# Bigbird attention and a top-2 mixture of experts in one kernel: zero fills moved to the middle batches, listed v rows by byte offset, keys issued ahead of values

## The chip, the cores and the metric

The kernel runs on one core of a Trainium2 chip. The metric is device time in microseconds (us) of one execution. Three timed runs of the kernel before stand beside one profiled execution; the profile's clock of TensorE is the granted one, as a share of full speed (2.4 GHz; the lower level is 1.2 GHz, 0.50).

## The reference

```python
def _attn_ref(q, k, v, sampled_blocks):            # B, H, S, D = 4, 8, 768, 64; 24 blocks of 32
    scores = scale * np.matmul(q, k.transpose(0, 1, 3, 2))
    mask = np.abs(blk_i - blk_j) <= window             # window = 1 block
    mask = mask | (blk_i == 0) | (blk_j == 0) | (blk_i == n_blocks - 1) | (blk_j == n_blocks - 1)
    for qb in range(n_blocks):
        for kb in sampled_blocks[qb]:                  # 3 listed blocks for each query block
            mask[qb * block:(qb + 1) * block, kb * block:(kb + 1) * block] = True
    ...                                                # masked softmax, then attn @ v

def _moe_ref(x, w_gate, w_noise, noise, w1, w2):       # N, D, E, F = 3072, 512, 8, 1024
    noisy_logits = x @ w_gate + np.log1p(np.exp(x @ w_noise)) * noise
    ...                                                # top 2 of 8 experts, softmax of the two
    h = np.maximum(x[mask] @ w1[e], 0.0)
    out[mask] += top2_w[mask, k, None] * (h @ w2[e])
```

The attention's output, 4 batches x 768 rows of 512 numbers, is the input x of the experts.

## The kernel before, in words

**Attention.** A batch b has 6 tiles t of 128 query rows, and each tile has two items f (four heads each); four more items "g" of a batch serve the first and the last block, which see everything. `steps()` walks 64 items in a software pipeline: in one step it scores the item two ahead (PE L238, then max and exp on DVE and ACT), turns the present one (PE transposes, L304), multiplies the one before with v (`av`, PE L326), and makes the output rows of the one before that (`high` on ACT L383, `low` on POOL L390). Two steps later `turn_x` transposes these rows on PE (L397). Rows of the first and last tile of a batch (x tile `xe`) also need the "g" result: POOL makes its low half (`xg`, L371), DVE copies it into `xe` (L376), and PE turns `xe`.

Every engine executes its instructions in the order in which the program writes them; nothing reorders them later. What sets the order is the code of `steps()`, and a table `plan` by step number, in which the last batch's extra work and the experts' first loads are put.

**Queues.** SP issues all plain DMAs, in program order. The DMAs use eight completion semaphores in turn (DMAHW0 to DMAHW7), and each waits for the one eight issues before it, which had the same semaphore. For each tile (b, t) SP issues: the query tile q (256 KB), a store of finished x rows (256 KB, L589, it waits for POOL's `low`), a TENSOR_LOAD of the listed block numbers into registers (L155), and in two halves the tile's v: one DMA of window rows per half (`vw`, up to 384 KB, L212) and the listed rows, 64 KB each (L216; 12 to a tile, 9 for t = 0 and 5). Half 1 of a tile is written one step behind half 0. v lies in three buffers (`va`, `vb`), two in the last batch; a tile's DMAs wait until PE's `av` of the buffer's last user is done. Ahead of every listed DMA stands register arithmetic (the "ISA" rows below, FUSED_REGOPS in the trace) that makes an address of a block number.

POOL does, in one stream: `weigh` (L224: two small copies of `known` into the columns of va and vb behind the 512 v columns), `prefetch_k` (kc copies L196 and L197: listed and neighbouring key blocks of a tile, which `scores` reads), `scale_k` (L176, each sixth of the next batch's keys kk), `low`, and all indirect DMAs. `load_k` (SP L164) brings the next batch's keys in six pieces.

**Zero fill.** The output is built by scattered additions, so 8 DMAs of 768 KB (L1284) fill it with zeros. They are in the plan at steps 49 to 57, in the last batch; their source is x tile 2, which POOL clears for it, and then a piece of `xg` of the experts.

**Experts.** Behind the attention come units of up to 816 token rows (expert products L1006, L1045, L1092, L1101). Rows are gathered by POOL (L948), transposed by SP's DMA (`xpose`, L958), and the running output is gathered too (`gather_prev`, POOL L966). Unit 0's gathers and transposes begin inside the last batch's steps.

Of the kernel before, what the change touches and what calls it, by code (L numbers as in the profile page):

```python
# [9 lines left out]
F32 = mybir.dt.float32  # L10
# [3 lines left out]
U32 = mybir.dt.uint32  # L14
U16 = mybir.dt.uint16
AF = mybir.ActivationFunctionType
ALU = mybir.AluOpType
AX = mybir.AxisListType
PSUM = bass.MemoryType.PSUM
P = 128  # L20
# [7 lines left out]
C = 816  # L28
# [5 lines left out]
OVC = OVT * P  # L34
NSLOT = NV * OVC
BIGIDX = 1 << 20
EW = 8
NC = E * EW
SW = 16384.0
FAST = 5  # L40
# [6 lines left out]
class Attention:  # L47
# [3 lines left out]
    def __init__(self, tc, qt, qg, kt, vx, vw, vg, sampled, H, D):  # L51
        self.tc, self.nc = tc, tc.nc
        self.qt, self.qg, self.kt, self.vx, self.vw, self.vg, self.sampled = qt, qg, kt, vx, vw, vg, sampled
        self.B, self.T = qt.shape[:2]
        self.H, self.D = H, D
        self.NP = H // 2
        self.S = self.T * P
        self.NB = self.S // 32
        self.W = D + 4
        self.HD = H * D  # L60
        self.HW = H * self.W
        self.late_ = (self.B - 1) * self.T
        self.items = []
        for b in range(self.B):
            q = [("q", b, t, f) for t in range(self.T) for f in range(2)]
            g = [("g", b, i, par) for i in range(2) for par in range(2)]
            self.items += g[0:2] + q[0:1] + g[2:3] + q[1:2] + g[3:] + q[2:] if b == 0 else q[0:1] + g[0:3] + q[1:2] + g[3:] + q[2:]
        self.st = {}

    def open(self, ctx, early, ident):  # L70
        tc, nc = self.tc, self.nc
# [12 lines left out]
        J = self.NJ  # L84
# [12 lines left out]
        nc.vector.tensor_copy(self.ident16, self.ident)  # L97
        nc.vector.memset(self.known, 1.0 / XS)

    def open_x(self, ctx):  # L100
# [9 lines left out]
    def blocks(self, mi):  # L110
        nc, NB = self.nc, self.NB
# [4 lines left out]
        t = lambda name, dt=F32, n=3: mi.tile([1, NB, n], dt, name=name)  # L116
        r = t("rf")
# [7 lines left out]
        bi = mi.tile([1, NB], F32, name="bi")  # L125
        nc.gpsimd.iota(bi, pattern=[[1, NB]], base=0, channel_multiplier=0, allow_small_or_imprecise_dtypes=True)
        u, w = t("du"), t("dw")
        nc.vector.tensor_tensor(u, r, bi[:, :, None].to_broadcast([1, NB, 3]), op=ALU.subtract)
# [9 lines left out]
        self.mi = self.const.tile([1, NB * 3], I32, name="mr")  # L138
        nc.vector.tensor_tensor(self.mi.rearrange("p (b k) -> p b k", k=3), r, w, op=ALU.subtract)
        ones = mi.tile([1, P], F32, name="on")  # L140
# [60 lines left out]
    def prefetch_v(self, b, t, half):  # L201
        nc, HD, J = self.nc, self.HD, self.NJ
        i = self.which(b, t)
        va, vb = self.va[i], self.vb[i]
        self.st["v", b, t] = va, vb
        js = self.real(t)
        first = t * J + js[0]
        if half == 0:
            self.unlisted = self.numbers(self.mi[0:1, 3 * first:3 * (first + len(js))], mybir.EngineType.SP, self.NB)
        js = [j for j in js if j // 2 == half]  # L210
        part = lambda x: x.rearrange("p (j c) -> p j c", j=J)[:, js[0]:js[-1] + 1]
        nc.sync.dma_start(va[0:96, js[0]:js[-1] + 1, 0:HD], part(self.vw[b, t]))  # L212
        vv = self.vx[b].rearrange("(n p) c -> n p c", p=32)
        for j in js:
            for n, d in enumerate((va[96:128, j], vb[0:32, j], vb[32:64, j])):
                nc.sync.dma_start(d[:, 0:HD], vv[bass.ds(self.unlisted[3 * (t * J + j - first) + n], 1)].rearrange("o p c -> (o p) c"))  # L216

# [213 lines left out]
    def steps(self, router, done, background):  # L431
# [7 lines left out]
        for k in range(-2, n + 7):  # L439
# [37 lines left out]
            if new[0] == "q" and new[1] + 1 < B:  # L477
                i = 2 * new[2] + new[3] - 1
                if i == 2:
                    self.load_g(new[1] + 1)  # L480
                    self.load_ends(new[1] + 1)
                if 2 <= i <= 7:
                    self.scale_k(new[1] + 1, i - 2, 6, nc.gpsimd)
            if new[0] == "q" and new[3] == 1 and nk < len(tg):
# [13 lines left out]
            while nv < len(tg) and (self.after(nv) < 0 and k > 0 or old[0] == "q" and old[3] == 1 and  # L498
# [5 lines left out]
                nv += 1  # L504
            if new[0] == "q" and new[1] + 1 < B and 0 < 2 * new[2] + new[3] <= 6:
                self.load_k(new[1] + 1, 2 * new[2] + new[3] - 1, 6)
            background(k, 3)
# [284 lines left out]
class Experts:  # L792
# [167 lines left out]

    def gather_prev(self, u):
        nc = self.nc
        r = self.st["u", u]
        for c in () if self.plain(u) else self.chunks(u):
            m = self.rows_of(u, c)
            nc.gpsimd.indirect_dma_start(  # L966
                out=self.pv[0:m, c, :], out_offset=None, in_=self.out,
                in_offset=bass.IndirectOffsetOnAxis(ap=r["gi"][0:m, c:c + 1], axis=0),
                bounds_check=self.N - 1, oob_is_err=False)
# [275 lines left out]
@with_exitstack  # L1245
def kernel(ctx, tc, qt, qg, kt, vx, vw, vg, sampled_blocks, gates, noise, w1, w2, out):
    nc = tc.nc
# [9 lines left out]
    ex = Experts(tc, router, w1, w2, out, x_dram)  # L1257
    att = Attention(tc, qt, qg, kt, vx, vw, vg, sampled_blocks, H, DM // H)
    late, early, left, right, first = (ExitStack() for _ in range(5))
# [18 lines left out]

    def spare():
        return att.xs[2].rearrange("p n a c -> p (n a c)")[:, 0:512].bitcast(F32)  # L1280

    def fill_out(i):
        z = spare() if i < 4 else ex.xg[:, C // P, 0:512].bitcast(F32)
        nc.sync.dma_start(out[i * 384:(i + 1) * 384].rearrange("(p n) (h d) -> p (n h) d", p=P, d=256),  # L1284
                          z[:, None, :].to_broadcast([P, 3 * DM // 256, 256]))

# [5 lines left out]

    at(PER * 3 + 1, lambda: nc.gpsimd.memset(spare(), 0.0))
    for i in range(8):
        at(PER * 3 + 1 + i + i // 4, fill_out, i)
    for i in range(3):
# [65 lines left out]
    def front(u, f):  # L1362
# [29 lines left out]
        if u >= FAST - 1:  # L1392
            e = ex.units[u][1]
            if u == FAST - 1:
                for c in ((0, 1), (2, 3), (4, 5), (6,))[f] if f < 4 else ():
                    ex.xpose(u + 1, c)
            do(u, FRONT[f])
            if nn:
                do(u, FRONT_ROWS[f])
# [47 lines left out]
    for u in range(nu):  # L1447
        left_ = ex.rows(u)[1]
        n = ex.count(u)
        ex.layer1(u, lambda f: front(u, f))  # L1450
        for k, c in enumerate(ex.chunks(u)):
            ex.mm2(u, c)
            if left_ and k == min(2, n - 1):
                ex.turn(u, n - 1)
            back(u, k, n)
        if u + 1 < nu:
            ex.gather_prev(u + 1)
        if u == 2:
            second.close()
            ex.open_sums(right)  # L1460
# [4 lines left out]

_INS = ['qt', 'qg', 'kt', 'vx', 'vw', 'vg', 'sampled_blocks', 'gates', 'noise', 'moe_w1', 'moe_w2']
_OUTS = [((3072, 512), 'float32')]
# [46 lines left out]
```

## Time and profile before

| | us |
|---|---|
| three runs | 861.11, 861.96, 867.26 (median 861.96) |
| the profiled execution | 867.49 |
| its span | 865.6 |
| PE busy in the span | 795.9 (92%) |
| DVE, ACT, POOL busy | 567.7, 388.4, 375.2 |
| mean granted clock | 0.959 |

Read it as two programs one behind the other: the attention with the router up to 318.68 us of the span, where the chain of work shows the first expert product (L1006), and then the experts, in which PE hardly stops. The change touches DMAs and small instructions of the first part. There PE's gaps, what ended each of them, and the time at which SP and POOL come to the work that PE waits for are what is to be read.

### The profile page before, as it was taken

How to read it: one execution, taken by the hardware profiler on the slowest of the kernel's cores; microseconds unless marked ns; L12 is line 12 of the kernel's file. 1: busy time of each engine (PE TensorE's matmuls, PEld its weight loads, DVE VectorE, ACT ScalarE, POOL GpSimd, SP SyncE). 2: the span in 40 equal slices, each digit the busy share in tenths (PEclk: the TensorE clock that was granted, in tenths of full speed). 3: DMA queues.
4: the chain of work that ended last, by engine and by line, in shares of the span. 5: the costliest groups of instructions: out<-in, count | busy, mean ns of one | idle time of the engine just before them, and what ended most of it. 6: DMA issues, size and time to landing. Idle time of an engine off the chain costs nothing.

```text
span 865.6 us, 25234 instructions
## 1 busy us (share of the span) xinstructions
PE 795.9 (92%) x9823; PEld 488.4 (56%) x9823; DVE 567.7 (66%) x1197; ACT 388.4 (45%) x722; POOL 375.2 (43%) x656
## 2 busy tenths in 40 slices
PE   8999789988967759999999879999999999999996
PEld 4566557666646547466586444554554554554552
DVE  7767767798797418752133268688698697796631
ACT  5869738858744325321023222552552542633510
POOL 5584379388554230141235316516426336322311
PEclk8999989999988769999999979999999999999999
DMA  7776676786688876764179939639639539523301
GB/s 226 205 209 179 200 202 186 201 233 192 213 246 271 208 173 171 195 185 96 52 174 208 188 102 235 203 97 228 190 105 237 185 100 242 164 79 117 102 28 52
DMA packets 119844, 148.88 MB, mean 172 GB/s; under 512 B 69516, under 2 KB 76301, under 8 KB 119715
## 3 DMA queue, kind: packets, MB, share of 16 engines
q1 hardware_dynamic: 107490, 109.22, 47.8%
q0 software_dynamic: 12224, 37.96, 13.9%
q8 instruction: 79, 1.29, 0.7%
q14 instruction: 51, 0.41, 0.2%
HBM read 107.28 MB, written 26.15 MB: 154 GB/s over the span
## 4 chain that ended last, share of the span: by engine, by line
PE 75%; DVE 9%; issue 6%; SPq 2%; DMA 2%; POOL 2%; ACT 2%; POOLq 1%; DVEq 0%; ACTq 0%
PE pc L1092 29%; PE pa L1045 10%; PE ps L238 6%; PE pa L1006 6%; PE pd L1045 5%; PE po L326 4%; PE pd L1006 3%; PE ps L304 3%; PE pc L1101 3%; PE pc L1045 2%; DVE m L277 2%; SPq L958 1%; PE po L349 1%; PE ps L292 1%; PE po L397 1%
## 5 line engine op out<-in xcount | busy, mean ns | idle before, releaser
L1092 PE MATMUL pc<-w,hh 128*128 128x512 f16 x768 | 228.4, 379 | 0.0
L1125 POOL DMA_INDIRECT out_dram<-y,r_xT x46 | 66.4, 1444 | 216.0 <-DVE y L1124 182.6
L1092 PE MATMUL pc<-w,hl 128*128 128x512 f16 x384 | 145.5, 379 | 0.0
L1092 PEld LDWEIGHTS <-hh 128*128 128x128 f16 x768 | 74.5, 98 | 86.4
L1045 PEld LDWEIGHTS <-w 128*128 128x128 f16 x840 | 82.2, 98 | 63.1
L280 ACT ACTIVATE p<-ps,m 128x256 f32<-128x256 f32 x192 | 75.2, 477 | 55.6 <-DVE m L277 54.9
L277 DVE TENSOR_REDUCE m<-ps 128x2 f32<-128x512 f32 x96 | 61.7, 684 | 32.3 <-PE ps L238 32.3
L1014 ACT ACTIVATE hh<-pa 128x408 f16<-128x408 f32 (+2 forms) x60 | 26.3, 447 | 123.2 <-PE pa L1006 111.9
L196 POOL COPY kc<-kk 128x128 f32 x264 | 68.1, 295 | 15.0 <-PE ps L238 7.7
L238 PE MATMUL ps<-kc,q 64*32 64x256 f32 x1536 | 64.3, 404 | 10.0 <-POOL kc L197 8.2
L896 DVE SCALAR_TENSOR_TENSOR w<-wraw,w 128x1024 f16<-128x1024 f32 (+1 forms) x58 | 65.3, 1128 | 10.5 <-ACT w L892 10.5
L326 PE MATMUL po<-va,ptr 128*32 128x68 f32 x1536 | 56.9, 233 | 13.2 <-DMA va<-in_vx_dram 9.6
L1017 DVE SCALAR_TENSOR_TENSOR hl<-pa,hh 128x408 f16<-128x408 f32 (+2 forms) x60 | 30.2, 504 | 54.1 <-ACT hh L1014 54.1
L948 POOL DMA_INDIRECT xg<-x_rows,r_xT x46 | 57.6, 1253 | 14.7 <-issue 14.4
L1092 PEld LDWEIGHTS <-hl 128*128 128x128 f16 x384 | 37.5, 98 | 45.3
L966 POOL DMA_INDIRECT pv<-out_dram,r_xT x44 | 48.0, 1090 | 32.9 <-issue 26.3
L326 PE MATMUL po<-vb,ptr 128*32 128x68 f32 x1536 | 55.0, 230 | 6.4 <-issue 5.4
L892 ACT ACTIVATE w<-wraw 128x1024 f16<-128x1024 f32 (+1 forms) x58 | 56.4, 975 | 6.7 <-DMA wraw<-in_moe_w_dram 6.7
L1124 DVE SCALAR_TENSOR_TENSOR y<-pc,r_xT,pv 128x512 f32<-128x512 f32 x37 | 27.8, 750 | 47.3 <-PE pc L1092 47.3
L326 PEld LDWEIGHTS po<-va,ptr 128*32 128x32 f32 x1536 | 39.2, 114 | 27.7 <-DMA va<-in_vw_dram 10.1
L304 PE MATMUL ps<-r_ident,p 128*128 128x128 f32 x384 | 54.6, 287 | 0.0
L1006 PE MATMUL pd<-xta,w 128*128 128x408 f16 (+1 forms) x144 | 46.8, 333 | 8.3 <-DVE hl L1017 8.2
(230 smaller groups left out, 1593.1 us busy)
## 6 DMA issues: line engine op xcount, KB each, us to landing
wraw<-in_moe_w_dram SPq DMA_DIRECT2D x64, 512.0 KB, 3.8
va<-in_vw_dram SPq DMA_DIRECT2D x40, 384.0 KB, 4.5
vb<-in_vx_dram SPq DMA_DIRECT2D x176, 64.0 KB, 3.1
q<-in_qt_dram SPq DMA_DIRECT2D x24, 256.0 KB, 3.5
va<-in_vx_dram SPq DMA_DIRECT2D x88, 64.0 KB, 3.5
kk<-in_kt_dram SPq DMA_DIRECT2D x18, 256.0 KB, 3.2
x_rows<-x SPq DMA_DIRECT2D x16, 256.0 KB, 4.2
out_dram<-x SPq DMA_DIRECT2D x4, 768.0 KB, 7.6
```

The costliest lines, as they stand in the source:

```text
L196: nc.gpsimd.tensor_copy(kc[:, j, :, 3 + n], flat[:, bass.ds(self.listed(blk, n), P)].rearrange("p (n c) -> p n c", c=32))
L238: mm = lambda o, l, r: nc.tensor.matmul(o, l, r, start=True, stop=True, skip_group_check=True)
L277: nc.vector.tensor_reduce(m[:, par], s[par].rearrange("p (e c) -> p e c", e=2), axis=AX.X, op=ALU.max, negate=True)
L280: nc.scalar.activation(p[:, 2 * e + par], s[par][:, 256 * e:256 * e + 256], AF.Exp, bias=m[:, par, e:e + 1])
L304: nc.tensor.transpose(t[:, e, c], p[:, 2 * e + par, P * c:P * c + P], self.ident)
L326: nc.tensor.matmul(o[32 * j:32 * j + 32, h], d[:, h % 2, h // 2, x, 32 * j:32 * j + 32], self.values(v[:, self.slot(t, j)], 4 * f + h), st ...
L896: self.nc.vector.scalar_tensor_tensor(lo, t, WS, hi, op0=ALU.mult, op1=ALU.subtract)
L948: nc.gpsimd.indirect_dma_start(out=self.xg[0:m, c + self.place(u)], out_offset=None, in_=self.x_dram[0:nr], in_offset=bass.IndirectOffsetO ...
L1006: nc.tensor.matmul(ph[:, 0:m], w[:, wt, slot, kb % 2 * P:kb % 2 * P + P], r["xt"][:, kb, a, o:o + m], start=i == 0, stop=i == last)
L1045: nc.tensor.matmul(o, w[:, wt, slot, s * P:s * P + P], mv(s, a), start=i == 0 and p in tail, stop=i == 5, skip_group_check=True)
L1092: nc.tensor.matmul(py, h[:, f, o], w(f)[:, x], start=i == 0, stop=i == last)
L1125: d = nc.gpsimd.indirect_dma_start(out=self.out, out_offset=bass.IndirectOffsetOnAxis(ap=r["ix"][0:m, c:c + 1], axis=0), in_=y[0:m], in_of ...
```

## The change

- The 8 zero fills go from steps 49 to 57 to steps 19, 22, ..., 40 (batches 1 and 2), one every third step. Their source is a new tile `zero` that DVE clears once at the start.
- Listed v rows are addressed by byte offsets. The numbers that SP loads are already block x 65,536; v comes as one tensor per batch (vx0 to vx3), and source and target of the DMA are seen as bytes (`bitcast(U8)`).
- The numbers that SP loads for tiles t = 3, 4 and 5 stay in registers over the batches (KEEP), so 9 of 24 TENSOR_LOADs go.
- `load_k` is written ahead of the step's v instead of behind it, and `scale_k` one step later (i - 3 in place of i - 2).
- Unit 4's `gather_prev` is written inside the loop of unit 4's front work rather than behind the previous unit.

```diff
+        self.RB = 32 * self.HD * 4
+        self.held_v = {}
...
+        self.zero = self.const.tile([P, 256], F32, name="zero")
+        nc.vector.memset(self.zero, 0.0)
...
-        nc.vector.tensor_tensor(self.mi.rearrange("p (b k) -> p b k", k=3), r, w, op=ALU.subtract)
+        nc.vector.scalar_tensor_tensor(self.mi.rearrange("p (b k) -> p b k", k=3), w, -float(self.RB), rb, op0=ALU.mult,
+                                       op1=ALU.add)
...
         if half == 0:
-            self.unlisted = self.numbers(self.mi[0:1, 3 * first:3 * (first + len(js))], mybir.EngineType.SP, self.NB)
+            self.unlisted = self.held_v.get(t)
+            if self.unlisted is None:
+                self.unlisted = self.numbers(self.mi[0:1, 3 * first:3 * (first + len(js))], mybir.EngineType.SP,
+                                             self.NB * self.RB)
+                if t in KEEP:
+                    self.held_v[t] = self.unlisted
...
-        vv = self.vx[b].rearrange("(n p) c -> n p c", p=32)
+        rows = self.vx[b].rearrange("s c -> (s c)").bitcast(U8)
         for j in js:
             for n, d in enumerate((va[96:128, j], vb[0:32, j], vb[32:64, j])):
-                nc.sync.dma_start(d[:, 0:HD], vv[bass.ds(self.unlisted[3 * (t * J + j - first) + n], 1)].rearrange("o p c -> (o p) c"))
+                at = self.unlisted[3 * (t * J + j - first) + n]
+                nc.sync.dma_start(d[:, 0:HD].bitcast(U8), rows[bass.ds(at, self.RB)].rearrange("(p c) -> p c", p=32))
...
                 i = 2 * new[2] + new[3] - 1
+                if 0 <= i < 6:
+                    self.load_k(new[1] + 1, i, 6)
...
-                if 2 <= i <= 7:
-                    self.scale_k(new[1] + 1, i - 2, 6, nc.gpsimd)
+                if 3 <= i <= 8:
+                    self.scale_k(new[1] + 1, i - 3, 6, nc.gpsimd)
...
-            if new[0] == "q" and new[1] + 1 < B and 0 < 2 * new[2] + new[3] <= 6:
-                self.load_k(new[1] + 1, 2 * new[2] + new[3] - 1, 6)
...
     def fill_out(i):
-        z = spare() if i < 4 else ex.xg[:, C // P, 0:512].bitcast(F32)
...
-                          z[:, None, :].to_broadcast([P, 3 * DM // 256, 256]))
+                          att.zero[:, None, :].to_broadcast([P, 3 * DM // 256, 256]))
...
-    at(PER * 3 + 1, lambda: nc.gpsimd.memset(spare(), 0.0))
     for i in range(8):
-        at(PER * 3 + 1 + i + i // 4, fill_out, i)
+        at(PER + 3 + 3 * i, fill_out, i)
...
+                if f > 3:
+                    ex.gather_prev(u, ex.chunks(u)[2 * f - 8:2 * f - 6])
...
-        if u + 1 < nu:
+        if u + 1 < nu and u + 1 != FAST - 1:
             ex.gather_prev(u + 1)
```

Two places show how instructions stand. The first is POOL at the turn from batch 0 to batch 1: `weigh` (L224, COPY va and vb) for tiles (1, 0), (1, 1) and (1, 2), between them `low` of the last rows of batch 0 (L390) and `xg` (L371), with the semaphores that each waits for. Before:

```order
L224 COPY va_96<-known 128x3x32
L224 COPY vb_99<-known 128x3x32
L390 TENSOR_TENSOR x_978<-xr,x_978 128x2x128 [waits Activation_49] x2
L224 COPY va_97<-known 128x4x32 [waits PE_49]
L224 COPY vb_100<-known 128x4x32 [waits PE_49]
L390 TENSOR_TENSOR xe<-xr,xe 128x2x128 [waits Activation_49] x2
L371 TENSOR_TENSOR xg<-xr,xg 128x2x128 [waits DVE_49,Activation_49]
L224 COPY va_98<-known 128x4x32 [waits PE_49,Pool_49]
L224 COPY vb_101<-known 128x4x32 [waits PE_49,Pool_49]
```

The same place in the changed kernel (weigh is L239 there, low L405, xg L386):

```order
L239 COPY va_96<-known 128x3x32 [waits DMAHW7_49,DMAHW4_49]
L239 COPY vb_99<-known 128x3x32 [waits DMAHW5_49,DMAHW6_49,DMAHW1_49,DMAHW0_49]
L405 TENSOR_TENSOR x_981<-xr,x_981 128x2x128 [waits Activation_49] x2
L239 COPY va_97<-known 128x4x32 [waits DMAHW4_49,DMAHW7_49,DMAHW0_49,PE_49]
L239 COPY vb_100<-known 128x4x32 [waits DMAHW2_49,DMAHW5_49,DMAHW1_49,DMAHW6_49,DMAHW0_49,PE_49]
L405 TENSOR_TENSOR xe<-xr,xe 128x2x128 [waits Activation_49] x2
L386 TENSOR_TENSOR xg<-xr,xg 128x2x128 [waits DVE_49,Activation_49]
L239 COPY va_98<-known 128x4x32 [waits DMAHW6_49,DMAHW3_49,DMAHW7_49,PE_49,Pool_49]
L239 COPY vb_101<-known 128x4x32 [waits DMAHW4_49,DMAHW1_49,DMAHW5_49,DMAHW0_49,DMAHW7_49,PE_49,Pool_49]
```

The order is unchanged; what is new is that both copies of each `weigh` wait for DMAs of SP: seen as bytes, the listed rows' target counts as touching the columns that `weigh` writes, so it waits for the listed rows of both halves of its own tile. The same holds for every tile of every batch.

The second place is SP between the last listed row of tile (1, 2) and the first of (1, 3), around the keys (kk) of batch 2. Before:

```order
L216 ISA
L216 DMA vb_101<-in_vx_dram 32x512 [waits DMAHW0_49]
L164 DMA kk_102<-in_kt_dram 128x512 [waits DMAHW1_49]
L589 DMA x_rows<-xe 128x1024 [waits DMAHW2_49,DVE_49]
L589 DMA x_rows<-xe 128x1024 [waits DMAHW3_49,DVE_49,Pool_49]
L187 DMA q<-in_qt_dram 128x512 [waits DMAHW4_49,PE_49]
L164 DMA kk_102<-in_kt_dram 128x512 [waits DMAHW5_49]
L169 DMA qg_106<-in_qg_dram 128x256 [waits DMAHW6_49]
L172 DMA ends_108<-in_vg_dram 64x512 [waits DMAHW7_49]
L155 TENSOR_LOAD mr
L212 DMA va_96<-in_vw_dram 96x2x512 [waits DMAHW0_49,PE_49]
```

And in the changed kernel:

```order
L231 DMA vb_101<-in_vx_dram 32x2048 [waits DMAHW0_49]
L173 DMA kk_102<-in_kt_dram 128x512 [waits DMAHW1_49]
L604 DMA x_rows<-xe 128x1024 [waits DMAHW2_49,DVE_49]
L604 DMA x_rows<-xe 128x1024 [waits DMAHW3_49,DVE_49,Pool_49]
L1295 DMA out_dram<-zero 768x1x256 [waits DMAHW4_49]
L173 DMA kk_102<-in_kt_dram 128x512 [waits DMAHW5_49]
L196 DMA q<-in_qt_dram 128x512 [waits DMAHW6_49,PE_49]
L173 DMA kk_102<-in_kt_dram 128x512 [waits DMAHW7_49]
L178 DMA qg_106<-in_qg_dram 128x256 [waits DMAHW0_49]
L181 DMA ends_108<-in_vg_dram 64x512 [waits DMAHW1_49]
L226 DMA va_96<-in_vw_dram 96x2x512 [waits DMAHW2_49,PE_49]
```

The arithmetic row ahead of each listed DMA and this tile's TENSOR_LOAD are gone, the first zero fill has come in, and a third piece of kk stands ahead of the v of (1, 3). On POOL the first `scale_k` of batch 2's keys now stands behind the kc copies of tile (1, 3), where it stood ahead of them. POOL's rows from the last batch's steps on are in the same order in both kernels, the `gather_prev` of unit 4 included; so are all of PE's and ACT's, while DVE has two instructions more.

## Rows read from the trace of the kernel before

**Rows 1.** Chain of waits, 290 to 325 us (start, length, what)

```profile
296.31 2.04 SPq L958
...
298.45 1.27 SPq L958
...
301.63 3.13 DMA vb<-in_vx_dram
...
318.68 0.42 PE pa L1006
```

**Rows 2.** Timeline of PE, attention (start, us, engine, line, operation [idle before <-releaser])

```profile
86.14 0.28 PE L397 MATMUL po<-a_ident,xe 128*128 128x128 f16 x2 [0.67 <-DVE xe L376]
...
109.40 3.07 PE L238 MATMUL ps<-kc,q 64*32 64x256 f32 x32 [6.90 <-POOL kc L197]
...
163.05 0.82 PE L397 MATMUL po<-a_ident,xe 128*128 128x128 f16 x8 [0.67 <-DVE xe L376]
...
231.91 0.28 PE L397 MATMUL po<-a_ident,xe 128*128 128x128 f16 x2 [0.67 <-DVE xe L376]
...
292.96 0.40 PE L326 MATMUL po<-va,ptr 128*32 128x68 f32 x2 [5.68 <-DMA va<-in_vx_dram]
293.64 0.32 PE L326 MATMUL po<-va,ptr 128*32 128x68 f32 x1 [0.28 <-DMA va<-in_vx_dram]
...
304.89 0.26 PE L326 MATMUL po<-vb,ptr 128*32 128x68 f32 x2 [0.88 <-DMA vb<-in_vx_dram]
```

**Rows 3.** Waits, 0 to 330 us (us in total, times, longest)

```profile
POOL kk L176 <- DMA kk<-in_kt_dram: 35.7, 9, 13.8
...
PE po L326 <- DMA va<-in_vx_dram: 9.6, 4, 5.7
```

**Rows 4.** Busy time, granted clock and DMA share by stretch

```profile
100.00:110.00 10.00, 3.10 (x100) 2.08 (x84) 6.05 (x36) 3.69 (x9) 4.76 (x17) 0.75 0.78 222
```

**Rows 5.** Line L216, whole run (xcount: duration ns min/median/max, first and last start)

```profile
L216 SPq DMA_DIRECT2D vb<-in_vx_dram x176: 315/316/1822, 8.5 to 301.6; - x176
```

**Rows 6.** Timeline of SP, around tiles (3, 1) and (3, 4)

```profile
227.40 0.83 SPq L216 DMA_DIRECT2D vb<-in_vx_dram  x2
...
277.04 0.36 SPq L589 DMA_DIRECT2D x_rows<-x  x1
280.62 0.34 SPq L212 DMA_DIRECT2D va<-in_vw_dram  x1
```

**Rows 7.** Line L155, whole run

```profile
L155 SPq TENSOR_LOAD <-mr x24: 745/1023/3427, 5.2 to 290.3; - x24
```

**Rows 8.** Line L1284, the zero fills, whole run

```profile
L1284 SPq DMA_DIRECT2D out_dram<-xg x4: 552/576/1126, 252.8 to 275.8; - x4
...
DMA to landing us min/median/max: 5.2/6.4/7.6
```

**Rows 9.** Line L216, end of tile (1, 1)

```profile
L216 SPq DMA_DIRECT2D vb<-in_vx_dram x6: 315/320/1122, 85.5 to 91.0; - x6
...
DMA to landing us min/median/max: 1.8/1.9/1.9
```

**Rows 10.** Timeline of POOL, turn to batch 1 and last batch

```profile
74.31 0.29 POOL L224 COPY va<-known 128x128 f32<-128x128 f32 x1
...
83.67 0.67 POOL L371 TENSOR_TENSOR xg<-xr,xg 128x256 f16<-128x256 f32 x1 [1.71 <-ACT xg L370]
...
275.34 1.26 POOL L948 DMA_INDIRECT xg<-x_rows,r_gi  x1 [0.18 <-issue]
```

**Rows 11.** Line L216, end of tile (2, 1)

```profile
L216 SPq DMA_DIRECT2D vb<-in_vx_dram x6: 315/316/1047, 155.9 to 160.8; - x6
...
DMA to landing us min/median/max: 2.4/2.7/3.2
```

**Rows 12.** DMA issues, 262 to 306 us (KB each, median us to landing)

```profile
vb<-in_vx_dram SPq DMA_DIRECT2D x22, 64.0 KB, 4.7
...
xg<-x_rows,r_gi POOLq DMA_INDIRECT x5, 6.1
```

More of the change, by code (lines that the diff above doesn't have):

```diff
@@ L15 @@
 U16 = mybir.dt.uint16
+U8 = mybir.dt.uint8
 AF = mybir.ActivationFunctionType
@@ L35 @@
 NSLOT = NV * OVC
+KEEP = (3, 4, 5)
 BIGIDX = 1 << 20
@@ L126, in blocks @@
         nc.gpsimd.iota(bi, pattern=[[1, NB]], base=0, channel_multiplier=0, allow_small_or_imprecise_dtypes=True)
+        rb = t("rb")
+        nc.vector.tensor_scalar(rb, r, float(self.RB), None, op0=ALU.mult)
         u, w = t("du"), t("dw")
@@ L959, in xpose, with gather_prev @@
                                          in_=self.xg[:, c + self.place(u)])
-    def gather_prev(self, u):
+    def gather_prev(self, u, some=None):
         nc = self.nc
         r = self.st["u", u]
-        for c in () if self.plain(u) else self.chunks(u):
+        for c in () if self.plain(u) else (some or self.chunks(u)):
             m = self.rows_of(u, c)
@@ L1245, with kernel @@
 @with_exitstack
-def kernel(ctx, tc, qt, qg, kt, vx, vw, vg, sampled_blocks, gates, noise, w1, w2, out):
+def kernel(ctx, tc, qt, qg, kt, vx0, vx1, vx2, vx3, vw, vg, sampled_blocks, gates, noise, w1, w2, out):
     nc = tc.nc
@@ L1257 @@
     ex = Experts(tc, router, w1, w2, out, x_dram)
-    att = Attention(tc, qt, qg, kt, vx, vw, vg, sampled_blocks, H, DM // H)
+    att = Attention(tc, qt, qg, kt, (vx0, vx1, vx2, vx3), vw, vg, sampled_blocks, H, DM // H)
     late, early, left, right, first = (ExitStack() for _ in range(5))
@@ L1277 @@
     UB = 9
-    def spare():
-        return att.xs[2].rearrange("p n a c -> p (n a c)")[:, 0:512].bitcast(F32)
     def fill_out(i):
-        z = spare() if i < 4 else ex.xg[:, C // P, 0:512].bitcast(F32)
         nc.sync.dma_start(out[i * 384:(i + 1) * 384].rearrange("(p n) (h d) -> p (n h) d", p=P, d=256),
-                          z[:, None, :].to_broadcast([P, 3 * DM // 256, 256]))
+                          att.zero[:, None, :].to_broadcast([P, 3 * DM // 256, 256]))
     plan = {}
@@ L1463 @@
     overflow(tc, router, w1, w2, out, x_dram, table)
-_INS = ['qt', 'qg', 'kt', 'vx', 'vw', 'vg', 'sampled_blocks', 'gates', 'noise', 'moe_w1', 'moe_w2']
+_INS = ['qt', 'qg', 'kt', 'vx0', 'vx1', 'vx2', 'vx3', 'vw', 'vg', 'sampled_blocks', 'gates', 'noise', 'moe_w1', 'moe_w2']
 _OUTS = [((3072, 512), 'float32')]
@@ L1487 @@
     vx[:, :S] = v.transpose(0, 2, 1, 3).reshape(B, S, H, D // 4, 4).transpose(0, 1, 3, 2, 4).reshape(B, S, H * D)
-    inputs["vx"] = vx
+    inputs.update((f"vx{b}", vx[b]) for b in range(B))
     near = _np.arange(0, S, 32)[:, None] + _np.arange(-32, 64)
```

## The prediction, made before the changed kernel ran

> **What bounds the kernel now.** I read four views in this order. The chain of waits comes first: at 318.68 us the first expert product starts [rows 1]. PE carries the rest of the span, and none of its instructions moves there, so the experts' part stays as it is, and only the 319 us ahead of it can change. Then PE's timeline there: the reader should look for the idle time in brackets. One stall is at the turn from batch 0 to batch 1, 6.90 us that POOL's kc copies end at 109.40 [rows 2]; behind it stands a POOL instruction that waited up to 13.8 us for the next batch's keys [rows 3]. The others are in the last batch: PE waits 9.6 us in four places for listed rows of v [rows 3], 5.68 of them at 292.96, and 0.88 at 304.89 [rows 2], 10.5 together. The clock shows the cost behind a stall: 0.75 on average from 100 to 110 us [rows 4], that is, half of that stretch at 1.2 GHz. The third view is SP, the queue that is late in all of these: two listed DMAs take 0.83 us, so they start 0.51 us apart [rows 6], though one issue takes 0.316 [rows 5]. The fourth is POOL, because there the order of instructions shows something that no row of before has: `weigh` now waits for the listed rows of its own tile.
>
> **The change part by part.** Times are against the profiled execution (867.49 us), 5.5 above the median of the three runs; a difference counts alike for both.
>
> *Listed rows.* Of the 0.51 us between two of them, 0.316 is the issue; the rest, 0.19, is arithmetic, moves and waiting. The arithmetic goes, moves and part of the waits stay, since eight DMAs may be open and each lands only after some 2.7 us [rows 11]. Bounds 0 and 0.19; I take the middle, 0.09 a row.
>
> *Kept numbers.* Nine loads of a median 1.02 us [rows 7] leave SP, three in each of batches 1, 2 and 3: 3.1 us a batch (at least 2.2, by the shortest row). The Trainium skill, page "DMA: Bandwidth & Descriptors", section "Latency and other measured facts", gives such a load a floor of about 600 ns; the shortest row here is 745, so the trace stays above it. By the page the three would free 1.8 us and the time below would come to 860.
>
> *Fills.* SP's issue of one takes 0.55 us at least, and it lands after 5.2 to 7.6 us [rows 8]. SP meets it again eight issues later, 8 x 0.51 = 4.1 us on, and waits there for the rest. So a fill costs SP between 0.55 us, if something else holds SP anyway, and 0.55 + 7.6 - 4.1 = 4.1. In the new places the fills go one at a time, as the quickest here did, so I take 0.55 + 5.2 - 4.1 = 1.7. Four lie ahead of the last row of tile (2, 1), four more ahead of (3, 1)'s.
>
> *Keys first.* The kc copies of tile (1, 3) no longer stand behind `scale_k`, and so not behind the late keys. The stall of 6.90 goes, and with it some lost clock: 0 to 2.5 us, since half of the 10 us ran at half rate [rows 4]; I take 1.5. That is -8.4.
>
> *The new wait, turn to batch 1.* POOL ran `weigh` of (1, 1) at 74.31 [rows 10]; the last listed row of that tile was issued at 91.0 and landed in 1.8, at 92.8 [rows 9]. Behind it on POOL stand two `low`, `xg`, the next `weigh` and the kc copies, and PE turns `xe` when `xg` is done: 84.34 on POOL [rows 10], 86.14 on PE [rows 2], 1.8 later. SP is late from tile (0, 3) on; from there to the end of (1, 1) it issues 54 listed rows, 54 x 0.09 = 4.9 us earlier, so the rows land at 87.9. Then come 0.5 for two copies and 3 x 0.67 on POOL, and 1.8 to PE: `xe` is turned at 92.2 in place of 86.14, 6.1 late (11 late if rows get no quicker, 1 if they gain 0.19). The turn gains 8.4 - 6.1 = 2.3. `weigh` of (1, 2) then holds the kc copies too, but PE comes to their scores 6 us later than it did, and I cost that at nothing; without that cover it is up to 3.
>
> *Turn to batch 2.* (2, 1) landed at 160.8 + 3.2 = 164.0 [rows 11]. SP by then has saved 120 x 0.09 = 10.8 and 3.1 of loads, and paid 4 x 1.7 = 6.8: 7.1 earlier, 156.9. Adding 2.5 and 1.8, PE can turn `xe` at 161.2 where it did at 163.05 [rows 2]. PE is thus ahead by 1.9 at most there, not 2.3.
>
> *Turn to batch 3.* (3, 1)'s last row was issued at 227.9 [rows 6], landing at 230.6 with the 2.7 of (2, 1). SP is earlier by 7.1 + 66 x 0.09 + 3.1 - 6.8 = 9.3, so `xe` could be turned at 225.6 against 231.91 [rows 2]: no wait. PE keeps its 1.9.
>
> *Last batch.* Without the load between 277.40 and 280.62 [rows 6] (3.2), one fill (0.6), 12 x 0.09 and rows that land in 4.7 [rows 12] and not in 2.7, tile (3, 4), which PE got at 293.64 [rows 2], would be there 6.9 earlier, at 286.7. But `weigh` of (3, 4) then stands ahead of the first gathers of unit 0 on POOL, which went at 275.34 [rows 10] and now go at 287.3; a gather takes 1.26 there and lands in 6.1 [rows 12], at 294.7, the next 1.3 later. SP's two transposes of 2.04 and 1.27, at 296.31 and 298.45 [rows 1], wait for them, and half 1 of (3, 5) is written behind these: SP reaches it at about 298.0 and not at 299.7. PE's last wait for v ends with it: 1.7 gained of the 10.5.
>
> *The rest.* Unit 4's `gather_prev` keeps its place in POOL's order: nothing. The clearing of `zero` is one small DVE instruction at the start, and POOL loses a clearing; both under 1 us.
>
> **Sum**: -1.9 - 1.7 = -3.6: 863.9 for the profiled execution, and 858.4 against the median 861.96; I say **858.5 us**. The likeliest case's own range is 851 to 866.
>
> **Rivals.**
>
> *The stalls simply go (26%).* If SP gains more, `weigh` has nothing to wait for: with 0.19 a row and 0.55 a fill, (1, 1) lands at 82.5 and `xe` comes 1 us late; the last batch's 10.5 go as well if the gathers are not what holds (3, 5). -7.4 - 10.5 = -18, 844 us. For it: SP's lateness ends each of those stalls. Against it: the new wait stands in the built order of every tile.
>
> *Fills and the new wait together (slower, 16%).* One mechanism at one place, the turn to batch 3: fills push (3, 1) back, POOL waits in `weigh`, and PE for `xe`. At 4.1 us a fill SP is 8 x 4.1 - 186 x 0.09 - 6.1 = 10.0 later, (3, 1) lands at 240.6 and `xe` is turned at 244.9, 13 late: with the last batch's 1.7 back, 873. It decides from 3.8 us a fill, where +8.6 is passed. For it: DMAs already fill 0.78 of the engines' time from 100 to 110 [rows 4]. Against it: a fill alone landed in 5.2. On this bears the page "DMA: Bandwidth & Descriptors" of the Trainium skill, section "Queues, rings and completion order": an engine takes descriptors in ring order, and the semaphore's increment lands only after every earlier write of that engine. By it, v rows behind a fill would be reported with the fill, which makes this rival more likely; no row here shows two such DMAs apart.
>
> *The listed rows get no quicker (10%).* Then the change does not do what byte offsets should. (1, 1) lands at 92.8, `xe` is turned 11.0 late there; at (2, 1) SP is 6.8 - 3.1 = 3.7 later and at (3, 1) 7.4: 230.6 + 7.4 + 4.3 - 231.91 = 10.4 late, 870.7 with the 1.7 back. For it: issue and landing with eight open may be what spaces the rows.
>
> **Chances.** The forecast has 48%. About 1% (8.6 us) is what a measurement can tell from no change: under 853.3 or over 870.6. Faster by more: most of the first rival and a little of the forecast, 0.27. Slower by more: most of the second, half of the third, 0.19. Within: 0.54. The range runs from 844, the first rival, to 872, near the two others.
>
> **What would show it.** In the changed trace POOL's idle time before `weigh` should be ended by DMAs of listed rows, above all at (1, 1), (2, 1) and (3, 4); the 6.90 at PE L238 should be gone, and PE's idle time before `xe` (0.67 now) be several us at the first turn. Listed pairs should start 0.42 apart, fills land in 5 to 6 us, nine loads be missing, and the first gathers go after 285. Wrong would be: `weigh` that finds its rows landed, listed rows still 0.5 apart, or a change in the experts' part beyond the run's spread.

## The result and the profile after

The changed kernel takes 873.5 us (median of five runs, 864.66 to 877.18) against 861.96 (five runs, 854.09 to 867.26). The ratio is 1.0123, 95% interval 1.0081 to 1.0165: slower by 1.2%, where 858.5 was forecast and 872 was the range's end. The ratios here and below leave out runs more than 1.5% above the quickest of their kernel; the medians do not.

The profiled execution of after happens to be the quickest of its five, 864.66 us with a span of 862.9, and that of before, 867.49, as long as its longest. The two traces must therefore be read by part. The first expert product, at 318.68 before [rows 1], starts at 324.95, 6.3 us later; behind it the experts take 537.9 us in place of 546.9. PE's, POOL's and SP's instructions there are in the same order, and most of the difference is one stall near 503 us. Before, in the timeline of PE:

```profile
503.39 0.50 PE L1006 MATMUL pd<-xta,w 128*128 128x408 f16 x1 [8.19 <-DVE hl L1017]
```

and after:

```profile
502.82 0.33 PE L1021 MATMUL pd<-xta,w 128*128 128x408 f16 x1 [1.74 <-DVE hl L1032]
```

The stall ends at nearly the same time in both, although the experts began 6.3 us apart. Whether it makes up for such a loss in most executions is not shown, with one profile of each kernel; the medians lie 11.5 us apart, so the 6.3 us do not account for all of the slow-down either. What the change moved stands ahead of 325 us, and there its cost is looked for. When PE begins `av` of a batch's first tile, by its timeline:

| PE begins | before | after | difference | forecast |
|---|---|---|---|---|
| av of (1, 0) | 81.3 | 85.8 | +4.5 | 0 |
| av of (2, 0) | 158.1 | 168.9 | +10.8 | -2.3 |
| av of (3, 0) | 227.1 | 241.2 | +14.1 | -1.9 |
| first expert product | 318.7 | 325.0 | +6.3 | -3.6 |

The first three batches lose 14 us, and the last gives 8 back. One execution of each is compared here, which is coarse: in five of the runs below (e2, e5, e9, e13 and e14), whose programs are alike up to there, av of (1, 0) begins between 79.0 and 83.6, so the first row's 4.5 is no more than their spread. The timeline of PE after, with the lines that answer to [rows 2] (line numbers have moved: 238 to 253, 397 to 412, 326 to 341):

```profile
50.78 0.62 PE L253 MATMUL ps<-kc,q 64*32 64x256 f32 x4 [0.31 <-POOL kc L206]
...
54.25 1.05 PE L253 MATMUL ps<-kc,q 64*32 64x256 f32 x20 [0.54 <-POOL kc L206]
...
95.79 1.13 PE L412 MATMUL po<-a_ident,xe 128*128 128x128 f16 x8 [5.79 <-DVE xe L391]
...
115.23 1.21 PE L253 MATMUL ps<-kc,q 64*32 64x256 f32 x32
...
246.43 0.82 PE L412 MATMUL po<-a_ident,xe 128*128 128x128 f16 x8 [1.00 <-DVE xe L391]
...
288.54 0.42 PE L341 MATMUL po<-va,ptr 128*32 128x68 f32 x8 [1.18 <-POOL va L239]
...
310.96 0.55 PE L341 MATMUL po<-va,ptr 128*32 128x68 f32 x8 [6.46 <-POOL va L239]
...
324.95 0.43 PE L1021 MATMUL pa<-xta,w1s 128*128 128x320 f16 x1 [1.17 <-ACT r_xT L413]
```

The stall of 6.90 us at 109.40 is gone: the same scores, counted through PE's instructions, start at 115.23 with no idle time, but 5.8 us later. In its place PE waits 5.79 us for `xe` at 95.79, in batch 0 for kc copies, of which it uses each the moment it is made (50.78 to 54.25, about half a microsecond each), and in the last batch 6.46 us for `weigh` itself at 310.96. The view of waits, 0 to 330 us, names the cause (us in total, times, longest):

```profile
POOL va L239 <- DMA va<-in_vx_dram: 40.1, 11, 7.3
POOL va L239 <- DMA vb<-in_vx_dram: 35.4, 7, 7.7
...
PE po L412 <- DVE xe L391: 10.6, 4, 5.8
...
PE po L341 <- POOL va L239: 7.6, 2, 6.5
```

75 us of POOL's time go into waiting for listed rows ahead of these copies; [rows 3] had no such line. POOL's timeline shows three of these places, tiles (0, 3), (1, 1) and (3, 4):

```profile
48.25 0.29 POOL L239 COPY va<-known 128x128 f32<-128x128 f32 x1 [7.28 <-DMA va<-in_vx_dram]
...
91.41 0.29 POOL L239 COPY va<-known 128x128 f32<-128x128 f32 x1 [7.73 <-DMA vb<-in_vx_dram]
...
93.88 0.67 POOL L386 TENSOR_TENSOR xg<-xr,xg 128x256 f16<-128x256 f32 x1
...
295.83 0.29 POOL L239 COPY va<-known 128x128 f32<-128x128 f32 x1 [5.48 <-DMA vb<-in_vx_dram]
...
297.66 1.26 POOL L963 DMA_INDIRECT xg<-x_rows,r_gi  x1 [0.28 <-issue]
```

At (1, 1) POOL stood for 7.73 us, `xg` ended at 94.55 (before: 84.34, [rows 10]), and the first gather of unit 0 went at 297.66 and not at 275.34.

SP did become quicker. Its timeline around the end of (1, 1), and its transposes in the last batch with the v rows behind them:

```profile
89.31 0.37 SPq L231 DMA_DIRECT2D va<-in_vx_dram  x1
89.84 0.78 SPq L231 DMA_DIRECT2D vb<-in_vx_dram  x2
...
302.74 3.48 SPq L973 DMA_TRANSPOSE xta<-xg  x2
306.26 0.57 SPq L226 DMA_DIRECT2D va<-in_vw_dram  x1
```

The pair of listed rows takes 0.78 where it took 0.83 [rows 6], and since the issue itself now takes 0.37, not 0.32, two rows start 0.41 apart (0.51 before) where nothing else holds them. Over the whole run, from one listed row to the next, the median is 0.46 (0.52 before). The fills, by their line (duration in ns min/median/max, and landing):

```profile
L1295 SPq DMA_DIRECT2D out_dram<-zero x8: 540/568/1342, 100.9 to 203.1; - x8
...
DMA to landing us min/median/max: 5.7/5.7/5.7
```

The profile has a landing for one fill of the eight, the one at 118.30: 5.7 us, where 5.2 was costed. What was not costed is what they do to others. DMA issues between 100 and 230 us, before (KB each, median us to landing):

```profile
vb<-in_vx_dram SPq DMA_DIRECT2D x82, 64.0 KB, 3.1
kk<-in_kt_dram SPq DMA_DIRECT2D x12, 256.0 KB, 3.0
q<-in_qt_dram SPq DMA_DIRECT2D x11, 256.0 KB, 3.6
```

and after:

```profile
vb<-in_vx_dram SPq DMA_DIRECT2D x72, 64.0 KB, 3.7
kk<-in_kt_dram SPq DMA_DIRECT2D x11, 256.0 KB, 4.7
q<-in_qt_dram SPq DMA_DIRECT2D x11, 256.0 KB, 5.2
```

The median query and piece of keys land 1.6 to 1.7 us later, a listed row 0.6. But the profile tells the landing of only some: of queries 3 before and 6 after, of keys 7 and 2. The queries after, by their line (landing of the six):

```profile
L196 SPq DMA_DIRECT2D q<-in_qt_dram x9: 378/817/1296, 102.5 to 199.1; - x9
...
DMA to landing us min/median/max: 3.6/5.2/7.1
```

The four of them that were issued within 4 us behind a fill land after 4.5 to 7.1 us, the two that had no fill within 9 us ahead of them after 3.6 and 3.8.

### The profile page after: what moved, and what is told of

Same layout as the page of the kernel before. It is cut to its first block, busy times and chain, and to the rows that moved or that the text cites. A ratio compares the mean times of both kernels' runs of the same rounds, so it can differ in the third digit from the quotient of the medians.

```text
span 862.9 us, 25034 instructions
## 1 busy us (share of the span) xinstructions
PE 798.9 (93%) x9823; PEld 489.7 (57%) x9823; DVE 569.9 (66%) x1199; ACT 389.0 (45%) x722; POOL 377.5 (44%) x655
## 5 line engine op out<-in xcount | busy, mean ns | idle before, releaser
L1021 PEld LDWEIGHTS <-w1s 128*128 128x128 f16 x432 | 42.7, 100 | 13.7 <-issue 1.3
```

## The experiments

Two theories were tested. W: what costs is POOL's new wait in `weigh`. F: what costs is the fills in batches 1 and 2. Ratios are to the kernel before on the same chip; e1 to e4 ran on one chip (before: median 862.6), e5 to e8 on a second one (875.5), e9 to e12 with a median of 876.7 and e13 and e14 with 875.2, so only ratios are compared. Each was profiled once.

| | what it is | ratio to before, 95% | first expert product, us |
|---|---|---|---|
| after | the change | 1.0123 (1.0081 to 1.0165) | 324.95 |
| e1 | change, weigh mostly left out | 0.9936 (0.9887 to 0.9984) | 319.36 |
| e2 | change, weigh ahead of v | 0.9990 (0.9948 to 1.0032) | 319.39 |
| e3 | change, fills back | 1.0051 (1.0010 to 1.0091) | 322.88 |
| e4 | change, rows as f32 | 1.0109 (1.0070 to 1.0148) | 325.04 |
| e5 | e2 and fills back | 0.9857 (0.9797 to 0.9916) | 310.36 |
| e6 | before, fills moved | 1.0087 (1.0049 to 1.0124) | 330.05 |
| e7 | before, keys first | 1.0019 (0.9983 to 1.0054) | 319.76 |
| e8 | e2, fills on ACT's queue | 1.0037 (1.0000 to 1.0075) | 325.38 |
| e9 | e5, fills behind the attention | 0.9981 (0.9945 to 1.0018) | 306.32 |
| e10 | e5 without kept numbers | 0.9913 (0.9880 to 0.9946) | 309.37 |
| e11 | e4 and fills back | 1.0005 (0.9972 to 1.0037) | 321.28 |
| e12 | e5 with the old order of keys | 0.9967 (0.9933 to 1.0000) | 319.07 |
| e13 | e5, fills in steps without keys | 0.9899 (0.9860 to 0.9937) | 310.86 |
| e14 | e5 again | 0.9931 (0.9897 to 0.9964) | 310.24 |

**e1, the wait taken away.** The copies are made once for each buffer. Behind the first three tiles the kernel leaves out the listed blocks' own weights, and nothing on POOL comes behind a v row there.

```diff
     def weigh(self, b, t):
+        if b * self.T + t > 2:
+            return
...
```

> The changed kernel, but the two small copies behind v (weigh) are made only for the first three tiles, so the weights of the listed blocks are wrong behind them. Theory W (POOL's new wait for the listed rows is what makes the changed kernel slower): POOL waits for no v, xe at the first turn comes within 1 us, PE's waits for POOL's weigh (7.6 us) and for xe (10.6 us) are gone, the attention ends at 300 to 312 us of the span (325 in the changed kernel, 319 before) and the time is 852 to 862. Rival F (the fills in batches 1 and 2 make SP late, POOL only passes it on): PE waits for v itself instead, the time stays at 868 to 876.

By the two ratios it is 1.9% below the change; but its ratio rests on six of twelve runs, and the median of all twelve, 862.47, is level with the kernel before, which makes it 1.2%. W holds: PE turns `xe` at 86.09, as before. But the attention ends at 319.36, not at 300 to 312, and the trace says why (timeline of PE):

```profile
86.09 0.28 PE L419 MATMUL po<-a_ident,xe 128*128 128x128 f16 x2 [0.67 <-DVE xe L398]
...
188.90 1.96 PE L260 MATMUL ps<-kc,q 64*32 64x256 f32 x32 [8.53 <-DMA q<-in_qt_dram]
```

There is a new stall of 8.53 us for the query tile in the turn to batch 3, near 189 us, which neither before nor after has, and which speaks for F as well; e5 and e6 test that.

**e2, the wait turned round.** Here `weigh` is written ahead of its tile's DMAs, with nothing left out.

```diff
+                i = self.which(*tg[nv])
+                self.st[("v", *tg[nv])] = self.va[i], self.vb[i]
+                self.weigh(*tg[nv])
                 self.prefetch_v(*tg[nv], 0)
                 halves.append(tg[nv])
-                marks += [(k + 1, self.weigh, nv, ()), (k + 1, self.spread, nv, (0,)), (k + 2, self.spread, nv, (2,))]
+                marks += [(k + 1, self.spread, nv, (0,)), (k + 2, self.spread, nv, (2,))]
```

> The changed kernel with weigh written ahead of its tile's v rows instead of behind them: POOL waits for no v row, but the listed rows on SP wait for POOL's copies. Theory W: 856 to 866, part of the gain goes to SP's wait for POOL. Rival F: 868 to 876 like the changed kernel.

Median 863.96: 1.3% below the change by the ratios, as W had it, but no quicker than the kernel before. SP's listed rows wait 2.2 us for POOL's `weigh`, in three places.

**e3, the fills put back, the wait kept.**

```diff
-        at(PER + 3 + 3 * i, fill_out, i)
+        at(PER * 3 + 1 + i + i // 4, fill_out, i)
```

> The changed kernel with the zero fills back at steps 49 to 57 (source still the cleared tile). Theory W: POOL's waits stay and the last batch gets its collision with the fills back: 868 to 882, no better than the changed kernel. Rival F: batches 1 and 2 lose nothing any more, the turn to batch 3 comes 10 us earlier, 856 to 864.

Median 867.46, between the two theories: 0.7% below the change. The intervals still touch (1.0091 and 1.0081), so that the fills cost in their new place even under the wait is likely, not shown, by this run. The wait's two large stalls are still there (timeline of PE):

```profile
97.19 1.14 PE L412 MATMUL po<-a_ident,xe 128*128 128x128 f16 x8 [5.32 <-DVE xe L391]
...
310.36 0.56 PE L341 MATMUL po<-va,ptr 128*32 128x68 f32 x8 [6.18 <-POOL va L239]
```

**e4, rows as f32.** The offset in the register still counts bytes, but source and target are f32 again.

```diff
-                nc.sync.dma_start(d[:, 0:HD].bitcast(U8), rows[bass.ds(at, self.RB)].rearrange("(p c) -> p c", p=32))
+                nc.sync.dma_start(d[:, 0:HD], rows[bass.ds(at, self.RB)].rearrange("(p c) -> p c", p=32).bitcast(F32))
```

> The changed kernel with the listed rows written as f32: the offsets are still bytes in registers, but the arithmetic row ahead of each listed DMA is back, and weigh waits for no DMA. Theory W: no wait in weigh, listed pairs start about 0.5 us apart, 852 to 864. Rival F: SP is even later than in the changed kernel, 874 to 882.

Median 871.66, between the two theories again. The wait is gone and the arithmetic row is back, and it is longer than it was (0.071 us at the median, 0.046 before), so that rows start 0.53 apart, not 0.51. What the one gives the other takes, and the fills remain. It is e6 with keys first and kept numbers added, and comes out near e6.

**e5, no wait and the fills back.** The diff is that of e2 and e3 together.

> Weigh ahead of v as in e2, and the zero fills back at steps 49 to 57: what is left of the change is byte offsets, kept numbers and keys first. Theory F2 (fills beside the keys and queries of batches 2 and 3 cost there what the last batch gains): PE's two stalls of 5 to 9 us near 109 and 189 us fall below 4, the last batch has about 6 us more of them, 854 to 861. Rival K (keys first only moves the wait for the keys by one tile, fills or not): both stalls stay over 4 us, 862 to 868.

Median 866.02 where before has 875.47, and the lowest ratio of all, on four of its six runs. The 8 us near 189 are gone; the stall at the first turn is not (timeline of PE):

```profile
108.32 1.96 PE L253 MATMUL ps<-kc,q 64*32 64x256 f32 x32 [4.78 <-POOL kc L205]
...
189.93 0.61 PE L412 MATMUL po<-a_ident,x 128*128 128x128 f16 x8 [2.31 <-DVE og L370]
```

So F2 is right about the turn to batch 3, and rival K about the first turn, where 4.78 of the 6.90 stay.

**e6, the fills alone.**

```diff
...
-        at(PER * 3 + 1 + i + i // 4, fill_out, i)
+        at(PER + 3 + 3 * i, fill_out, i)
```

> The kernel before with nothing changed but the fills, which go to steps 19 to 40 with the cleared tile as source. Theory F2: the stall near 109 us grows beyond 6.9, another over 4 us comes at the turn to batch 3, the last batch loses 5 to 8 of its 10.5: 860 to 868, no gain. Rival: the middle batches have room for 6 MB more, and the last batch's stalls just go: 850 to 856.

Slower by 0.9%, more than F2 had: the last batch's stalls for v do shrink, to 3.5 us in all, but PE comes to it 19 us later than before (it turns `xe` of batch 2 at 251.30, before at 231.91, [rows 2]). The timeline of PE has the two turns:

```profile
114.55 2.31 PE L240 MATMUL ps<-kc,q 64*32 64x256 f32 x32 [8.12 <-POOL kc L198]
...
196.30 3.19 PE L240 MATMUL ps<-kc,q 64*32 64x256 f32 x32 [8.26 <-DMA q<-in_qt_dram]
```

and SP's timeline shows how a fill stands ahead of the query that PE waits for at 196.30; below it the same place before, without a fill:

```profile
189.58 0.56 SPq L1285 DMA_DIRECT2D out_dram<-zero  x1
190.24 1.70 SPq L591 DMA_DIRECT2D x_rows<-xe  x2
192.03 1.14 SPq L189 DMA_DIRECT2D q<-in_qt_dram  x1
```

```profile
170.90 1.82 SPq L589 DMA_DIRECT2D x_rows<-xe  x2
172.81 0.40 SPq L187 DMA_DIRECT2D q<-in_qt_dram  x1
```

This one fill takes 0.56 us, and the query's issue behind it 0.74 more than before; the stores take no longer. The larger part of the 8.26 is that SP is late as a whole: from the same query of the batch ahead (at 108.75; before at 103.65) to this one it takes 83.3 us, with five fills in between, and 69.2 before. That is 2.8 us a fill.

**e7, keys first alone.** Two blocks moved, as in the diff of the change.

> The kernel before with nothing changed but load_k ahead of the step's v and scale_k a step later. Theory F2: without fills in front of them the keys land in 3.2 us and the 6.9 us near 109 shrink to 0 to 3: 855 to 860. Rival K: the wait is only moved to the next tile, 4 to 7 us there, 861 to 866.

No difference: the stall at the first turn stands at 114.12 with 8.01 us, now ended by the query's DMA and not by the kc copies. SP is late with everything there, and that query is issued at 107.7, before at 103.65: putting the keys ahead puts the query behind.

**e8, the fills on another queue.**

```diff
-        nc.sync.dma_start(out[i * 384:(i + 1) * 384]...
+        nc.scalar.dma_start(out[i * 384:(i + 1) * 384]...
```

> Weigh ahead of v as in e2, and the fills in the same steps, but issued by ACT's queue, not by SP's. If what a fill costs is SP's issue and its turn in the eight semaphores: keys and queries land 2 us earlier, 852 to 859. If it is the DMA engines' time, which all queues share: 861 to 867, as e2.

1.0037, no better than e2, and PE's waits for the query are longer still (timeline of PE):

```profile
116.31 1.96 PE L253 MATMUL ps<-kc,q 64*32 64x256 f32 x32 [11.98 <-DMA q<-in_qt_dram]
...
194.39 1.96 PE L253 MATMUL ps<-kc,q 64*32 64x256 f32 x32 [8.14 <-DMA q<-in_qt_dram]
```

But the run does not take the fill out of SP's way. The view of SP's waits has a line that after and e2 do not have (us in total, times, longest):

```profile
SPq L231 <- DMA out_dram<-zero: 15.7, 5, 6.4
```

A fill on ACT's queue still takes its turn in the same eight semaphores, and the listed row behind it waits on SP until ACT has come to issue the fill and the fill has landed: from 100.14 to 106.59 us for the fill issued at 101.50. So e8 does not separate SP's issue and semaphores from the time of the DMA engines; which of them a fill costs stays open.

**e9, the fills behind the attention.**

```diff
...
-        at(PER + 3 + 3 * i, fill_out, i)
+        at(NS + 3 + i // 4, fill_out, i)
```

> As e5 (weigh ahead of v, byte offsets, kept numbers, keys first), but all 8 fills are issued behind the last x store, where SP has nothing to issue for 11 us before the first expert product. Theory F2: in the attention no DMA waits for a fill any more, it ends 6 to 9 us earlier than in e5; what the fills cost the loads of the experts' weights behind them gives some of it back: 0.972 to 0.984 of the kernel before. Rival: the weights' loads come 10 us late and PE waits for them, 0.985 to 0.995.

The attention ends at 306.32, 4 us before e5's, and then the loss that the rival named takes nearly all of the gain: PE waits 13.46 us for the experts' weights, which SP issues behind the fills (timeline of PE):

```profile
306.32 0.43 PE L1024 MATMUL pa<-xta,w1s 128*128 128x320 f16 x1 [1.17 <-ACT r_xT L413]
...
332.54 0.43 PE L1024 MATMUL pd<-xta,w1s 128*128 128x320 f16 x1 [13.46 <-DVE hl L1035]
```

**e10, without kept numbers.** KEEP is empty.

> As e5 without the kept numbers: 24 TENSOR_LOADs as before. If the kept numbers bring what the rows say (9 x 1 us of SP's time, not all on the path): 0.3 to 0.8% slower than e5, 0.989 to 0.994 of the kernel before. If nothing waits for SP there: 0.986 like e5.

Between e5's two results (0.9857, 0.9931), and its attention ends 1 us earlier: no gain of the kept numbers can be told. This stays open.

**e11, kept numbers and keys first only.**

> Rows written as f32 as in e4 (arithmetic ahead of each listed DMA, weigh waits for no DMA) and the fills back at steps 49 to 57: kept numbers and keys first are what is left of the change. If byte offsets carry e5's gain: 0.995 to 1.003 of the kernel before. If the kept numbers carry it: 0.985 to 0.992.

1.0005: these two bring nothing that shows, but under rows that start 0.53 apart, as in e4, and so a little later than before's. What e5 has beyond it is the quicker rows, and `weigh` ahead of v.

**e12, e5 with the old order of keys.**

> As e5, but the keys in the old order: load_k behind the step's v, scale_k a step earlier. If keys first brings nothing (as alone in e7): 0.983 to 0.988 of the kernel before. If it needs the quicker rows to bring something: 0.990 to 0.996.

The ratio lies above both ranges. In the profiles the attention ends 9 us later than in e5, but this execution, 879.42 us, is the longest of its kernel but one, and the ratio's interval overlaps that of e5's repetition (e14, up to 0.9964): inconclusive, with a lean to the second reading, that keys first pays only when the rows are quick. At the first turn PE stands 2.36 us here, less than in e5.

**e13 and e14, where the fills stand.** In e13 the eight fills are in batches 1 and 2 as in the change, but in steps in which SP loads no keys.

```diff
...
-        at(PER + 3 + 3 * i, fill_out, i)
+        at(PER * (1 + i // 4) + 10 + 2 * (i % 4), fill_out, i)
```

> As e5, with the fills at steps 26, 28, 30, 32 and 42, 44, 46, 48: in batches 1 and 2 like the change, but in the steps in which SP loads no keys. If a fill in the middle costs because it stands ahead of the next batch's keys and queries: 0.982 to 0.990 of the kernel before, as e5 or better. If a fill costs anywhere in batches 1 and 2, since v is late there as well: 0.995 to 1.002, as e2.

> The kernel of e5 once more, beside e13 on the same chip: 0.980 to 0.991 of the kernel before.

0.9899 beside 0.9931: as e5, and below e2's 0.9990 (the intervals of e13 and e2 are apart, on two chips). Batches 1 and 2 take the 6 MB at no more cost than the last batch does; the steps with the next batch's keys and first queries are what costs. In PE's timeline the turn to batch 3 is down to 2.37 us, while the first turn, with no fill near it, keeps its stall:

```profile
108.79 1.96 PE L253 MATMUL ps<-kc,q 64*32 64x256 f32 x32 [6.91 <-POOL kc L205]
...
180.11 1.96 PE L253 MATMUL ps<-kc,q 64*32 64x256 f32 x32 [2.37 <-POOL kk L185]
```

These two stalls can be followed through all traces. At the turn to batch 3, with fills ahead of it and no wait in `weigh` (e1, e2, e4, e6, e8), PE stands 5.3 to 8.5 us; with the fills elsewhere (before, e5, e7, e9 to e12 and e14) 0 to 4.6. At the first turn the four programs that are alike up to there (e5, e9, e13, e14) stand 4.78, 1.77, 6.91 and 3.69 us. So one trace's stall at the first turn tells little of an edit.

e5, e10 and e13 beat both kernels, the kernel before by 0.7 to 1.4%.

## Why the prediction was wrong

**The new wait** was seen, and its mechanism held: at the first turn PE waited 5.79 us for `xe`. The 6.1 that was forecast is the lateness of the turn, which came out as 9.7 (95.79 against 86.14). The step that failed was to price the wait at the turns alone. "`weigh` of (1, 2) then holds the kc copies too ... and I cost that at nothing" was right at that place, but batch 0 was not looked at: `weigh` of (0, 3) waited 7.28 us, kc copies behind it came late, and batch 1 began 4.5 us late, which the spread between executions may have a part in. In the last batch PE waits for `weigh` directly, which the prediction had only as a delay of gathers: these went at 297.66 (forecast 287.3), and half 1 of (3, 5) at 306.26 (forecast 298.0). Taken away, the wait is worth 1.2% to 1.9% (e1, e2); the forecast had its whole price covered by what SP gained.

**SP's gain** was the sum that failed under both. "54 x 0.09 = 4.9 us earlier", "7.1 earlier" and "9.3" say when the last listed row of a tile goes out; the traces have, in us:

| last listed row of | before | forecast | after | e5 (no wait, fills back) | e2 (no wait, fills moved) |
|---|---|---|---|---|---|
| (1, 1) | 91.0 | 86.1 | 90.3 | 91.6 | 90.8 |
| (2, 1) | 160.8 | 153.7 | 163.7 | 156.1 | 166.6 |
| (3, 1) | 227.9 | 218.6 | 237.5 | 223.4 | 241.5 |

With neither wait nor fills SP is 2 to 5 us earlier at (2, 1) and (3, 1) (e5 and its repetition e14), where 13.9 and 22.9 were counted ahead of the fills' price. And the four and the eight fills ahead of these rows make SP 8.6 to 10.5 and 15.6 to 18.1 us later in e2 than in e14 and e5: 2.0 to 2.6 us a fill, not 1.7.

**The fills** were the other failed step. The term "a fill costs SP ... 0.55 + 5.2 - 4.1 = 1.7" was near for landing (5.7 in place of 5.2), but too small for SP as a whole, and it was applied to rows of v only. "No wait" at the turn to batch 3 fell with it: SP comes late to the query and the keys behind the fills, these land late as well, and PE waits for them, 8.26 us in e6. The rival "fills and the new wait together" had the time, 873, and had the fills push v back so that POOL waits in `weigh`; the runs show each cost without the other (e6 has no wait, e3 has no fills there), and without the wait the fills' goes through queries and keys. SP's lateness did come out as it had it (9.6 us at (3, 1), 10.0 in the rival), but at 2.0 to 2.6 us a fill, under its 3.8, with smaller gains beside them; and PE waits 1.00 us for `xe` at that turn, not 13, since it had lost the time earlier. So its 873 is in part luck. On the ordering rule of the Trainium skill ("DMA: Bandwidth & Descriptors", section "Queues, rings and completion order": an increment lands only after every earlier write of that engine, across its queues) the trace agrees in direction: queries issued within 4 us behind a fill land after 4.5 to 7.1 us, others after 3.6 and 3.8. Whether it is that rule or the engines' shared time was not told apart.

**Listed rows**: forecast 0.09 us a row, measured 0.10 in a free pair but 0.06 at the median of the run. Their worth, with the wait and the misplaced fills gone, is likely most of e5's 0.7 to 1.4%, since e11, without them, is at 1.0005; but e11 also has slower rows than before and `weigh` in its old place, so that this is argued, not shown.

**Keys first** failed as a step: -8.4 at the first turn was forecast, and in after the stall is indeed gone, but because PE comes there later (115.23 against 109.40). Where nothing else delays PE it stays, at 1.77 to 8.01 us in e5, e7, e9, e13 and e14, and 2.36 with the old order in e12. The chain of before had named the keys; behind them the query was just as late, since SP was.

**Kept numbers**: nine loads went as forecast; no run shows a gain. **Unit 4's `gather_prev`** was not run by itself; its instructions stand where they stood.

**The last batch** gave back 7.8 us (14.1 to 6.3), not 1.7. Counted in the same way against the kernel before, the other runs without fills there (e1, e2, e4, e6, e8, e9) get 7 to 12 back and those with them (e3, e5, e7, e10 to e12, e14) 0.5 to 6: the fills' place there was worth more than the 0.6 us and the quicker landing it was priced at. Why was not tested.

## What to carry to other kernels

A view of a tile in another type can make the planner see an overlap that is not there: compare what each instruction waits for, not only the order, and walk every place behind a new wait, the first batch included. When a large transfer is moved into a stretch that "has room", look at what is issued right behind it; in steps without keys the same bytes left that stall at 2.37 us. And a wait that one late transfer ends will be ended by the next late one, as long as the queue is late as a whole. A transfer that is issued from another engine may still hold the first queue, when both share their completion semaphores.

## What the runs showed of the hardware

A DMA whose source and target are seen as bytes, at an offset in a register, is issued in 0.365 to 0.370 us at the median; seen as f32 it takes 0.316, with an index (before) and with the same byte offsets (e4). The spacing of a free pair falls from 0.51 to 0.41 us all the same, as no arithmetic row stands ahead of it. Loads of 256 KB issued within 4 us behind a 768 KB write landed after 4.5 to 7.1 us (four), and away from one after 3.6 and 3.8 (two). With the writes on ACT's queue PE's waits for such loads were no shorter (11.98 and 8.14 us in e8), but there SP itself stood 15.7 us for the semaphores of these writes.
